# Soft-capped attention, then a max-out MLP, on one core: the scores of the left-over keys are issued ahead of the sums and values, and a third pair of PSUM banks holds scores in the first quad too

## The chip, the cores and the metric

The program runs on one core of one Trainium2 chip. The metric is device time in microseconds, from launch to the end of the program. The profile gives, for one execution, the span from its first to its last instruction. Engines: PE is TensorE's matmul, PEld its weight load, DVE VectorE, ACT ScalarE, POOL GpSimd, SP the engine whose queue issues most DMAs.

## The reference

```python
batch, n_heads, seq, head_dim = 8, 12, 448, 64          # q, k, v, float32
scores = cap * tanh((q @ k.T) / sqrt(64) / cap)          # cap = 30
attn = exp(scores - max(scores)); attn = attn / attn.sum(-1)
attn_out = attn @ v                                      # 8 x 12 x 448 x 64
x = attn_out.transpose(0, 2, 1, 3).reshape(3584, 768)
out = maximum(x @ w1, x @ w2) @ w_out                    # 3584 x 768, d_ff = 1024
```

The kernel leaves the maximum out of the softmax, since the cap bounds the scores. It uses max(a, b) = relu(a - b) + b: `wd_sb` holds w1 - w2, and `wm_sb` holds w2 @ w_out, so that the MLP is relu(x @ wd) @ w_out + x @ wm.

## The kernel before

**Work items.** Two heads of one batch make a pair, two pairs a quad `t` (0 to 23). Heads have 448 keys: three tiles of 128 keys (`j` = 0, 1, 2) and 64 keys that are left over. `scores(t, p)` issues, for pair p = 0 or 1 of the quad, three pairs of matmuls (one of each pair per head, each on half of the array's rows), and each such pair of matmuls fills a pair of PSUM banks that one tanh on ACT (L304) reads. `scores(t, 2)` does the left-over keys of both pairs: the left keys of two heads share one tile of 128, so it is two matmuls (L300), one pair of banks and one tanh. `ex(t, p)` is the exponential (L309) of all the tanhs of that part.

`total(t)` sums the exponentials over the keys with matmuls by a vector of ones (L343 and L347 in the early quads, L350 later), transposes on DVE (L352), takes the reciprocal (L354) and transposes back (L356) into `inv[t]`. `values(t)` is 32 matmuls of 32 columns each (L366, L372), into one pair of banks. `normalize(t, ps)` multiplies both banks by `inv[t]` on DVE (L387), which frees them.

**PSUM.** Eight banks: `s_psum` has two pairs, used in rotation by the scores and by `total`; `v_psum` has one pair, tile name `v`; `mm_psum` has two single banks for the MLP. With `scores(t, p, v_psum)` the third pair of score banks (`j` = 2) is the `v` pair; without it, all three `j` go through the two `s` pairs.

**Order.** It is written out by hand, and every engine runs its own queue in that order. The main loop makes one visit per quad `t`. In a visit the engines get, in this order: `scores(t+1, 0)`, then `ex(t, 2)`, fill, `scores(t+1, 1)`, then `ex(t+1, 0)`, fill, `total(t)`, `values(t)`, `scores(t+1, 2)`, `ex(t+1, 1)`, `normalize(t)`, the POOL casts for a later group, fill. Fill is `F(n)`: the next n matmuls from a queue of MLP work (`moe`, L399, L411 and L414, with DVE evacuations L403 and L418) or, early, of weight work (`turn_w2`, `premultiply`). A full visit calls F for 16 matmuls between the first and the second block of scores, for 24 from there to `total`, and for 5 at the end. What is left of the queue runs after the last visit.

Short names used below: S0, S1 and S2 are the matmuls of `scores(t+1, 0)`, `(t+1, 1)` and `(t+1, 2)`; T0, T1, T2 their tanhs; E0, E1, E2 the exponentials. On ACT a visit is T0, E2 of the quad at hand, T1, E0, T2, E1.

**Inputs.** q, k and v come in groups of three pairs (`load`, issued on SP), are cast to bf16 on POOL (in the visits, behind a copy `mark` at L629 that waits for `inv[t]`), and q and k are then transposed by a DMA (`cross`, L279) into `qkT`. The first two groups are transposed on TensorE instead.

Of the kernel before, what the change touches and what calls it, by code (L numbers as in the profile page):

```python
# [10 lines left out]
def kernel(  # L11
# [41 lines left out]
    v_psum = ctx.enter_context(tc.tile_pool(name="v_psum", bufs=1, space=PSUM))  # L53
# [170 lines left out]
    def subtract(c, eng=nc.vector):  # L224
        eng.tensor_sub(wd_sb[:, c, :], w1_in[c], w2b[:, c, :])
# [35 lines left out]
    def transposes(i):  # L261

        g, n = divmod(i, L)
        ps = mm_psum.tile([P, 512], f32, name="mm").bitcast(bf16)
        x = flat(g)[:, n, :]

        todo = [(j * D, (j % 3) * P + (j // 3) * 64) for j in range(6)]
        odd = i // NP % 2
        todo += [(Q0 + j * D, Q0 + (64 * j if not odd else 0 if j == 6 else 64 + 64 * j)) for j in range(R7)]
        for c, to in todo:  # L270
            for a in range(2):
                r = slice(64 * a, 64 * a + 64)
                nc.tensor.transpose(ps[r, to : to + 64], x[r, c : c + D], ident[r, r])
        nc.tensor.transpose(ps[:, NJ * P : Q0], x[:, NJ * P : Q0], ident)
        nc.vector.tensor_copy(qkT_of(g)[:, n, :, :].rearrange("p j c -> p (j c)")[:, : Q0 + S], ps[:, : Q0 + S])

    def cross(g):

        nc.sync.dma_start_transpose(  # L279
            out=qkT_of(g).rearrange("p n j c -> p (n j) c"), in_=kqf[g % 2].rearrange("p n j c -> p (n j c)")  # L280
        )
# [3 lines left out]
    def two_banks(pool):  # L285
        return pool.tile([P, 2, 512], f32, name="s" if pool is s_psum else "v")

    def scores(t, p, last=None):

        tanh[t, p] = att.tile([P, 2 * NJ, S], bf16, name="tanh")  # L290
        for j in range(NJ if p < 2 else 1):
            s = two_banks(last if last and j == NJ - 1 else s_psum)
            for m in range(2):
                i = 2 * t + (p if p < 2 else m)
                g = i // L
                k0 = qkT[g][:, i % L, :, :].rearrange("p j c -> p (j c)")
                o = Q0 + (64 * (i // NP % 2) if g >= NT else 0)
                qTn = k0[:, o : o + S]
                if p == 2:
                    nc.tensor.matmul(s[:, m, :S], k0[:, 3 * P : 4 * P], qTn)  # L300
                else:
                    r = slice(64 * m, 64 * m + 64)
                    nc.tensor.matmul(s[:, m, :S], k0[r, j * P : (j + 1) * P], qTn[r, :])  # L303
            nc.scalar.activation(tanh[t, p][:, 2 * j : 2 * j + 2, :], s[:, :, :S], AF.Tanh, scale=scale / cap)  # L304

    def ex(t, p):
        n = 2 * NJ if p < 2 else 2
        expo[t, p] = att.tile([P, n, S], bf16, name=f"expo{p}", bufs=2)
        nc.scalar.activation(expo[t, p], tanh[t, p][:, 0:n, :], AF.Exp, scale=float(cap))  # L309

    def e_of(t, ab, j):
        return expo[t, ab][:, 2 * j : 2 * j + 2, :]
# [24 lines left out]
    def total(t):  # L337

        ss = two_banks(s_psum)[:, 0, :]
        if t < NS:  # L340
            for j in range(NJ):
                for ab, h, r in HEADS:
                    nc.tensor.matmul(  # L343
                        ss[r, :S], ones[:, :32], e_of(t, ab, j)[:, h, :], start=(j == 0), stop=False
                    )
            for ab, h, r in HEADS:
                nc.tensor.matmul(ss[r, :S], ones2[:, h, :32], expo[t, 2][:, ab, :], start=False, stop=True)  # L347
        else:
            for ab, h, r in HEADS:
                nc.tensor.matmul(ss[r, :S], ones[:, :32], esum[t][:, 2 * ab + h, :], start=True, stop=True)  # L350
        st = att.tile([P, NB, 32], f32, name="st", bufs=1)
        nc.vector.transpose(st.rearrange("p b c -> p (b c)"), ss[:, :S])  # L352
        rs = att.tile([P, NB, 1], f32, name="rs", bufs=2)
        nc.vector.reciprocal(rs, st[:, :, 0:1])  # L354
        inv[t] = att.tile([P, S], f32, name="inv", bufs=2)
        nc.vector.transpose(inv[t].rearrange("p (b c) -> p b c", c=32), rs.to_broadcast([P, NB, 32]))  # L356

    def values(t):

        out = two_banks(v_psum)  # L360
        for u in range(2):
            ps = out[:, u, :]
            for j in range(NJ):
                for ab, h, r in HEADS:
                    g, n = divmod(2 * t + ab, L)
                    nc.tensor.matmul(  # L366
                        ps[r, :S], vp[g % 2][:, 2 * n + h, j, u::2], e_of(t, ab, j)[:, h, :],
                        start=(j == 0), stop=False,
                    )
            for ab, h, r in HEADS:  # L370
                g, n = divmod(2 * t + ab, L)
                nc.tensor.matmul(  # L372
                    ps[r, :S], vl[g % 2][:, n, 64 * h + u : 64 * h + 64 : 2], expo[t, 2][:, ab, :], start=False, stop=True
                )
        return out
# [3 lines left out]
    def x_of(t, u):  # L379
        b, q = divmod(t, 3)  # L380
        if b // 2 not in xT:
            xT[b // 2] = xpool.tile([P, NP, 2 * S], bf16, name="xT")
        return xT[b // 2][:, 2 * q + u, (b % 2) * S : (b % 2 + 1) * S]

    def normalize(t, ps):
        for u in range(2):
            nc.vector.tensor_mul(x_of(t, u), ps[:, u, :S], inv[t])  # L387
# [55 lines left out]
    def F(n):  # L443
        rate[1] += n * rate[0]
        while rate[1] >= 1 and fill_q:
            try:
                next(fill_q[0])
                rate[1] -= 1
            except StopIteration:
                fill_q.pop(0)  # L450
        if not fill_q:
            rate[1] = 0.0
# [35 lines left out]
    transposes(0)  # L488
    cast(nc.vector, 0, "k", 1, L)
    cast(nc.vector, 0, "q", 1, L)  # L490
    scores(0, 0)
    ex(0, 0)
    transposes(1)
    scores(0, 1)
    ex(0, 1)
    transposes(2)
    for _ in turn_w2(0):
# [35 lines left out]
    def extra(i):  # L533
        for f, a in todo[i]:
            f(*a)

    for _ in turn_w2(1):
        pass
    scores(1, 0)
    transposes(3)  # L540
    cast(nc.vector, 0, "v", halves=(0,))
    cast(nc.gpsimd, 1, "v")
# [28 lines left out]
    for t in range(1, NQ):  # L571
        i = 2 * t
        more = t + 1 < NQ
        if t > 1:
            F(24 if t == 2 else 0)
            if more:
                scores(t + 1, 0, v_psum)
            ex(t, 2)
            F(6)
        if t in crosses:  # L580
            cross(crosses[t])
        if t == 2:
            cast(nc.gpsimd, 3, "k")
            cast(nc.gpsimd, 3, "q")
            cross(3)
            for c in range(4, KC):
                subtract(c, nc.gpsimd)
        if t == 3:
            cast(nc.gpsimd, 3, "v")
        if t > 2:  # L590
            extra(i)
        if t > 1:
            F(2)
            add(t, 0, 0)
            F(3)
            add(t, 0, 1)
            F(3)
            add(t, 1, 0)
            F(2)
        if more:  # L600
            scores(t + 1, 1, v_psum)
            ex(t + 1, 0) if t > 1 else None
        F(3)
        add(t, 1, 1)
        F(4)
        if t == 2:
            cast(nc.gpsimd, 2, "v")
            load(3, "v")
        F(3)
        add(t, 0, 2)  # L610
        F(4)
        add(t, 1, 2)
        if t == 1:
            for c in range(4):
                subtract(c, nc.gpsimd)
        if t == 2:
            extra(4)
            extra(5)
        if t > 2:
            extra(i + 1)  # L620
        F(10)
        total(t)
        ps = values(t)
        if more:
            scores(t + 1, 2)
            ex(t + 1, 1)
        normalize(t, ps)
        if casts[t]:
            nc.gpsimd.tensor_copy(mark, inv[t][:1, :1])  # L629
            for g, what in casts[t]:  # L630
                cast(nc.gpsimd, g, what)
        if t % 3 == 2:
            fill_q.append(moe(t // 3))
        F(5)
# [34 lines left out]
```

## Time and profile before

| | |
|---|---|
| time, median of 3 runs | 371.25 us (370.80 to 371.84) |
| the profiled execution | 372.04 us, of which 370.3 us are its span |
| PE busy | 336.5 us, 91% of the span |
| ACT busy | 277.2 us, 75% |
| DVE busy | 227.2 us, 61% |
| POOL busy | 111.3 us, 30% |
| mean granted TensorE clock | 0.986 |

The visits of quads 3 to 22 begin and end near T2, which starts at 59.57 us for the first of them and at 317.62 us at the end of the last: 20 visits in 258.05 us. What lies ahead of that is the start (loads, transposes, weight work); what lies behind it is the last quad and the rest of the MLP, where ACT has nothing left to do. The share of an engine over the whole span is thus a mean over three quite different stages, and the visits have to be read on their own.

### The profile page before, as it was taken

The page shows a single profiled execution, that of the slowest core. Times are in us where ns is not written, and L with a number is a line of the kernel's source. Part 1 is how long each engine was busy: PE and PEld are TensorE (multiplying, and loading weights), DVE is VectorE, ACT ScalarE, POOL GpSimd, SP SyncE. Part 2 cuts the span into 40 slices and gives each one's busy share as a digit, 9 for nine tenths or more (in the row PEclk, how much of TensorE's full clock was granted, in tenths as well). Part 3 has the DMA queues.
Part 4 walks back from the last instruction along what each step waited for, and adds up shares of the span by engine and source line. Part 5 has one row for each costly group of instructions (what it writes and reads, how often), then busy time and mean ns, then how long its engine had stood idle before and what let it go on. Part 6 is the DMA issues. An engine that isn't in the chain of part 4 may idle for free.

```text
span 370.3 us, 6777 instructions
## 1 busy us (share of the span) xinstructions
PE 336.5 (91%) x2710; PEld 167.3 (45%) x2710; DVE 227.2 (61%) x410; ACT 277.2 (75%) x241; POOL 111.3 (30%) x172
## 2 busy tenths in 40 slices
PE   3679989999999998999999999999999999999996
PEld 2334544444444444454444444444444544455563
DVE  4225637857687655766676666867587666863421
ACT  3997677798889889788988988798898889500000
POOL 6652938324404421430332143034204400000000
PEclk9958999999999999999999999999999999999999
DMA  7999998984984399448946796759783512012022
GB/s 255 245 248 258 315 242 164 267 195 111 225 273 86 118 232 307 97 111 184 304 115 145 153 293 182 163 95 253 206 193 65 139 44 87 2 42 87 0 87 85
DMA packets 103199, 61.78 MB, mean 167 GB/s; under 512 B 62336, under 2 KB 98176, under 8 KB 103168
## 3 DMA queue, kind: packets, MB, share of 16 engines
q1 hardware_dynamic: 101216, 58.21, 60.8%
q0 software_dynamic: 1952, 3.15, 4.7%
q8 instruction: 21, 0.34, 0.4%
q14 instruction: 10, 0.08, 0.1%
HBM read 42.47 MB, written 11.01 MB: 144 GB/s over the span
## 4 chain that ended last, share of the span: by engine, by line
PE 52%; ACT 29%; DMA 12%; DVE 3%; issue 2%; SPq 0%; ACTq 0%; DVEq 0%
ACT tanh L304 17%; PE mm L414 14%; ACT expo L309 11%; PE mm L399 11%; PE mm L411 10%; DMA kr<-in_k_dram 8%; PE v L366 6%; DMA qkT<-kqf 3%; PE s L300 3%; PE v L303 2%; PE v L372 2%; PE s L350 2%; PE mm L243 2%; DMA osb<-in_moe_w_dram 1%; DVE gT L403 1%
## 5 line engine op out<-in xcount | busy, mean ns | idle before, releaser
L304 ACT ACTIVATE tanh<-s 128x896 bf16<-128x896 f32 x125 | 108.8, 914 | 43.0 <-PE s L300 33.4
L309 ACT ACTIVATE expo<-tanh 128x2688 bf16<-128x2688 bf16 (+1 forms) x72 | 140.3, 1950 | 0.8 <-PE v L366 0.6
L414 PE MATMUL mm<-wo_sb,gT 128*128 128x384 bf16 x448 | 85.5, 326 | 0.0
L399 PE MATMUL mm<-xT,wd_sb 128*128 128x448 bf16 x384 | 78.3, 353 | 0.8 <-DVE gT L403 0.7
L411 PE MATMUL mm<-wm_sb,xT 128*128 128x384 bf16 x336 | 65.8, 326 | 0.0
L418 DVE COPY osb<-mm 128x384 f32<-128x384 f32 x56 | 31.1, 555 | 56.5 <-PE mm L414 55.2
L414 PEld LDWEIGHTS <-gT 128*128 128x128 bf16 x448 | 42.8, 98 | 31.3 <-issue 3.6
L399 PEld LDWEIGHTS <-wd_sb 128*128 128x128 bf16 x384 | 36.5, 98 | 37.8 <-issue 6.1
L403 DVE TENSOR_SCALAR gT<-mm 128x448 bf16<-128x448 f32 x64 | 39.5, 621 | 19.9 <-PE mm L399 19.5
L303 PE MATMUL s<-qkT 64*128 64x448 bf16 x202 | 35.7, 373 | 15.9 <-ACT tanh L304 12.0
L629 POOL COPY mark<-inv 1x1 f32<-1x1 f32 x18 | 3.2, 178 | 154.3 <-DVE inv L356 137.0
L411 PEld LDWEIGHTS <-xT 128*128 128x128 bf16 x336 | 32.0, 98 | 24.2 <-issue 3.4
L303 PEld LDWEIGHTS <-qkT 64*128 64x128 bf16 x288 | 13.7, 94 | 58.6 <-issue 52.6
L304 ACT ACTIVATE tanh<-v 128x896 bf16<-128x896 f32 x43 | 39.7, 923 | 0.0
L366 PE MATMUL v<-expo,vp 128*32 128x448 bf16 x576 | 35.6, 353 | 0.0
L387 DVE TENSOR_TENSOR xT<-v,inv 128x448 bf16<-128x448 f32 x48 | 27.7, 619 | 4.7 <-PE v L372 2.0
L327 DVE TENSOR_TENSOR esum<-esum,expo 64x896 bf16<-64x896 bf16 x42 | 26.2, 623 | 7.1 <-ACT expo L309 6.4
L329 DVE TENSOR_TENSOR esum<-expo 128x896 bf16<-128x896 bf16 x42 | 28.3, 674 | 0.0
L331 DVE TENSOR_TENSOR esum<-esum,expo 128x896 bf16<-128x896 bf16 x42 | 26.8, 637 | 0.8
L352 DVE STREAM_TRANSPOSE st<-s 128x448 f32<-128x448 f32 x24 | 15.6, 649 | 17.7 <-PE s L350 15.9
L303 PE MATMUL v<-qkT 64*128 64x448 bf16 x86 | 15.6, 351 | 8.9 <-ACT tanh L304 8.9
L366 PEld LDWEIGHTS <-vp 128*32 128x32 bf16 x576 | 15.3, 97 | 10.0
(66 smaller groups left out, 258.5 us busy)
## 6 DMA issues: line engine op xcount, KB each, us to landing
kr<-in_k_dram SPq DMA_DIRECT2D x14, 576.0 KB, 6.8
qr<-in_q_dram SPq DMA_DIRECT2D x14, 576.0 KB, 6.9
vr<-in_v_dram SPq DMA_DIRECT2D x14, 576.0 KB, 5.0
out_dram<-osb SPq DMA_DIRECT2D x20, 384.0 KB, 4.2
out_dram<-osb SPq DMA_DIRECT2D x16, 192.0 KB, 3.5
osb<-in_moe_w_dram SPq DMA_DIRECT2D x4, 512.0 KB, 8.6
gT<-in_moe_w_dram POOLq DMA_DIRECT2D x6, 256.0 KB, 12.6
wo_sb<-in_moe_w_out_dram POOLq DMA_DIRECT2D x4, 384.0 KB, 16.1
```

What stands on the lines that cost most here:

```text
L303: nc.tensor.matmul(s[:, m, :S], k0[r, j * P : (j + 1) * P], qTn[r, :])
L304: nc.scalar.activation(tanh[t, p][:, 2 * j : 2 * j + 2, :], s[:, :, :S], AF.Tanh, scale=scale / cap)
L309: nc.scalar.activation(expo[t, p], tanh[t, p][:, 0:n, :], AF.Exp, scale=float(cap))
L329: nc.vector.tensor_add(d, e_of(t, ab, 0), e_of(t, ab, 1))
L331: nc.vector.tensor_add(d, d, e_of(t, ab, 2))
L366: nc.tensor.matmul(ps[r, :S], vp[g % 2][:, 2 * n + h, j, u::2], e_of(t, ab, j)[:, h, :], start=(j == 0), stop=False,)
L387: nc.vector.tensor_mul(x_of(t, u), ps[:, u, :S], inv[t])
L399: nc.tensor.matmul(ps[:, :S], wd_sb[:, c, f * P : (f + 1) * P], x[:, c, cs], start=(c == 0), stop=(c == KC - 1))
L403: nc.vector.tensor_relu(g[:, f, cs], ps[:, :S])
L411: nc.tensor.matmul(ps[:, : DM // 2], x[:, c, ts], wm_sb[:, c, hs], start=(c == 0), stop=False)
L414: nc.tensor.matmul(ps[:, : DM // 2], g[:, f, ts], wo_sb[:, f, hs], start=False, stop=(f == FC - 1))
L418: nc.vector.tensor_copy(osb[:, hs], ps[:, : DM // 2])
```

## The change

In every visit `scores(t+1, 2)` and its exponential's issue move ahead of `total(t)` and `values(t)`, and `normalize(t)` follows them directly. Separately, three of the scores in the start use the `v` pair for `j` = 2.

```diff
@@ the first quad
-    scores(0, 0)
+    scores(0, 0, v_psum)
     ex(0, 0)
     transposes(1)
-    scores(0, 1)
+    scores(0, 1, v_psum)
...
-    scores(1, 0)
+    scores(1, 0, v_psum)
...
@@ the end of a visit
         F(10)
-        total(t)
-        ps = values(t)
         if more:
             scores(t + 1, 2)
             ex(t + 1, 1)
-        normalize(t, ps)
+        total(t)
+        normalize(t, values(t))
         if casts[t]:
```

On TensorE the left-over scores (L300, into an `s` pair) are found, in the changed program, behind the fill and ahead of the sums. The piece shown is from the visit of quad 2, whose fill is weight work (L243) and whose sums are L343.

```order
 L243 LDWEIGHTS w2T
 L243 MATMUL mm<-wo_sb,w2T 128x384 [waits DVE_49]
+L300 LDWEIGHTS qkT
+L300 MATMUL s<-qkT 128x448 [waits Activation_49]
+L300 LDWEIGHTS qkT
+L300 MATMUL s<-qkT 128x448
 L343 LDWEIGHTS ones
 L343 MATMUL s<-expo_527,ones 32x448 [waits Activation_49]
```

The four rows stood behind the last matmul of the values (L372) before; in the rotation of the `s` pairs they now take the pair that the sums took, and the sums the other.

The next place is S0 of a visit, the first scores behind the values, on TensorE. First the rows before: `s` is a pair of `s_psum`, `v` the pair of `v_psum`, and the waits are on semaphores that ACT, DVE, a DMA or PE itself raise.

```order
L303 LDWEIGHTS qkT [waits DMAHW2_49]
L303 MATMUL s<-qkT 128x448 [waits DVE_49]
L303 LDWEIGHTS qkT
L303 MATMUL s<-qkT 128x448
L303 LDWEIGHTS qkT
L303 MATMUL s<-qkT 128x448 [waits Activation_49]
L303 LDWEIGHTS qkT
L303 MATMUL s<-qkT 128x448
L303 LDWEIGHTS qkT
L303 MATMUL v<-qkT 128x448 [waits DVE_49]
```

And the same rows of the changed program.

```order
L303 LDWEIGHTS qkT [waits DMAHW2_49]
L303 MATMUL s<-qkT 128x448 [waits Activation_49]
L303 LDWEIGHTS qkT
L303 MATMUL s<-qkT 128x448
L303 LDWEIGHTS qkT
L303 MATMUL s<-qkT 128x448 [waits DVE_49]
L303 LDWEIGHTS qkT
L303 MATMUL s<-qkT 128x448
L303 LDWEIGHTS qkT [waits DVE_49]
L303 MATMUL v<-qkT 128x448 [waits PE_49]
```

The first pair of S0 waited for the transpose of the sums on DVE and now waits for T2 on ACT; the second has it the other way round; the third waits for `normalize` on DVE in both, now at the weight load.

The third place is the start, on TensorE: the weight product into the `v` pair (L521, `premultiply_first`) between the scores of pairs (1, 0) and (1, 1).

```order
-L521 LDWEIGHTS w2T
-L521 MATMUL v<-wo_sb,w2T 128x384 [waits DMASW2_49]
+L521 LDWEIGHTS w2T [waits DMASW2_49]
+L521 MATMUL v<-wo_sb,w2T 128x384 [waits Activation_49]
 L521 LDWEIGHTS w2T
 L521 MATMUL v<-wo_sb,w2T 128x384
```

It now waits, besides the weights' DMA, for the tanh on ACT that reads the `v` pair of `scores(1, 0)`.

## The prediction, made before the changed kernel was run

> **What bounds the kernel now.** I read the page's engine shares and slices first, then three stretches of the trace by themselves, then who waits for whom, then one visit in order of time.
>
> The page's shares over the whole span, and its row of the granted clock in 40 slices:
>
> ```profile
> PE 336.5 (91%) x2710; PEld 167.3 (45%) x2710; DVE 227.2 (61%) x410; ACT 277.2 (75%) x241; POOL 111.3 (30%) x172
> PEclk9958999999999999999999999999999999999999
> ```
>
> Two stretches: the start, and the 20 visits (length, then busy time of each engine with its instructions, the granted clock, the DMA engines' share, GB/s):
>
> ```profile
> 0.00:48.97 48.97, 35.41 (x397) 18.66 (x398) 21.28 (x48) 35.18 (x30) 29.40 (x45) 0.90 1.06 259
> 64.10:317.60 253.50, 237.23 (x1876) 113.80 (x1876) 174.94 (x308) 225.20 (x197) 72.13 (x117) 1.00 0.67 171
> ```
>
> The start is full on the DMA side (share 1.06). In the visits PE is busy 237.2 of 253.5 us and ACT 225.2: both near full, neither quite. So each waits for the other somewhere. The waits, with total, times and longest:
>
> ```profile
> ACT tanh L304 <- PE s L300: 33.4, 23, 3.4
> PE s L303 <- ACT tanh L304: 12.0, 20, 1.6
> PE v L303 <- ACT tanh L304: 8.9, 20, 0.4
> PE mm L399 <- DVE gT L403: 0.7, 3, 0.3
> ```
>
> ACT waits for the left-over scores, which stand behind sums and values on PE; PE waits at S1 for the tanhs that free the banks. Is that a closed loop? ACT's T2 at the first visit, in the middle and at the last one:
>
> ```profile
> 59.57 0.92 ACT L304 ACTIVATE tanh<-s 128x896 bf16<-128x896 f32 x1 [1.87 <-PE s L300]
> 124.13 0.92 ACT L304 ACTIVATE tanh<-s 128x896 bf16<-128x896 f32 x1 [1.09 <-PE s L300]
> 317.62 0.92 ACT L304 ACTIVATE tanh<-s 128x896 bf16<-128x896 f32 x1 [1.54 <-PE s L300]
> ```
>
> Between the first and last there are 20 visits, 258.05 us, 12.90 each. PE through one of them (start, duration):
>
> ```profile
> 121.66 0.37 PE L350 MATMUL s<-esum,ones 128*32 128x448 bf16 x4
> 123.48 0.55 PE L300 MATMUL s<-qkT 128*128 128x448 bf16 x2
> 123.87 0.81 PE L414 MATMUL mm<-wo_sb,gT 128*128 128x384 bf16 x4
> 124.78 0.69 PE L303 MATMUL s<-qkT 64*128 64x448 bf16 x4
> 125.29 0.37 PE L303 MATMUL v<-qkT 64*128 64x448 bf16 x2
> 125.59 0.99 PE L411 MATMUL mm<-wm_sb,xT 128*128 128x384 bf16 x5
> 128.38 0.36 PE L303 MATMUL s<-qkT 64*128 64x448 bf16 x2
> 129.19 0.36 PE L303 MATMUL s<-qkT 64*128 64x448 bf16 x2 [0.44 <-ACT tanh L304]
> 130.00 0.36 PE L303 MATMUL v<-qkT 64*128 64x448 bf16 x2 [0.45 <-ACT tanh L304]
> 130.29 0.66 PE L411 MATMUL mm<-wm_sb,xT 128*128 128x384 bf16 x3
> 134.30 0.37 PE L350 MATMUL s<-esum,ones 128*32 128x448 bf16 x4
> ```
>
> From sum to sum 12.64 us. It is a loop: T2, E1 and T0 on ACT free S1's banks; PE then does 24 fill matmuls, sums, values and S2, and only then can T2 start again. In it ACT loses 1.09 us, so its own work is 11.55 us a visit.
>
> **The change: S2 ahead of the sums.** No instruction is added or removed in a visit.
>
> On ACT, S2 would be issued where the sums start now, 121.66, and E0 ends 1.09 us before 124.13, at 123.04. T2 then follows E0 with no wait. S2's bank comes free with the first tanh of T1; it is the bank that the sums take now, and their row at 121.66 has no wait. The sums then need the second tanh of T1, and the values, as now, the third.
>
> On PE, S1's second and third pair no longer wait, since T0 comes that much earlier. What a wait costs is read from starts, since the ends are modelled. Six score matmuls without a wait:
>
> ```profile
> 111.23 1.11 PE L399 MATMUL mm<-xT,wd_sb 128*128 128x448 bf16 x5
> 112.28 0.55 PE L303 MATMUL s<-qkT 64*128 64x448 bf16 x4
> 112.66 0.35 PE L303 MATMUL v<-qkT 64*128 64x448 bf16 x2
> 112.95 0.55 PE L399 MATMUL mm<-xT,wd_sb 128*128 128x448 bf16 x2
> ```
>
> First to third pair: 0.38 us, all six 0.67. In the visit above S1 takes 1.62 to the third pair: 1.24 us lost, more than the gaps of 0.44 and 0.45, because pairs that run apart don't overlap. The first and the last S1 of the 20:
>
> ```profile
> 64.11 0.36 PE L303 MATMUL s<-qkT 64*128 64x448 bf16 x2
> 65.44 0.36 PE L303 MATMUL v<-qkT 64*128 64x448 bf16 x2 [0.45 <-ACT tanh L304]
> 308.79 0.37 PE L303 MATMUL s<-qkT 64*128 64x448 bf16 x2
> 310.40 0.36 PE L303 MATMUL v<-qkT 64*128 64x448 bf16 x2 [0.44 <-ACT tanh L304]
> ```
>
> 0.95 and 1.23. Taken so, 14 of the 20 lose 1.19 to 1.24, five whose fill before S1 is L399 lose 0.78 to 0.90, and the first 0.95: **22.6 us** in all.
>
> S0 has a small wait too: in the visit above its third pair comes 0.51 after the first, not 0.38. The second pair waits for T2, which starts at 124.13 and ends at 125.05. That bank is then the sums' and early, and S0's first pair, which takes T2's bank, finds it free: 0.13 in 14 visits, **1.8 us**.
>
> Against these stands a wait that grows. S0's third pair needs the `v` banks, which `normalize` frees:
>
> ```profile
> 122.09 0.65 DVE L352 STREAM_TRANSPOSE st<-s 128x448 f32<-128x448 f32 x1 [1.39 <-PE s L350]
> 123.87 1.16 DVE L387 TENSOR_TENSOR xT<-v,inv 128x448 bf16<-128x448 f32 x2
> 127.41 1.73 ACT L304 ACTIVATE tanh<-s 128x896 bf16<-128x896 f32 x2
> ```
>
> `normalize` ends at 125.03, 3.37 after the sums start; with the 0.05 between the end of T0's second tanh (129.14) and the matmul that waits for it (129.19), 3.42. S2 (123.48 to 123.87, 0.39) no longer lies between, so PE reaches that pair 1.82 (sums, values) + 0.91 (five fill matmuls) + 0.38 = 3.11 after it: 0.31 of wait. Where the five are L399 (111.23 to 112.28, 1.05) it is 0.17; that is six visits. 14 x 0.31 + 6 x 0.17 = **5.4 us**. Bounds: nothing, if the weight load ahead covers it; another 20 x 0.65 = 13 us, if DVE came to the sums late by as much as L352 itself takes. DVE stood idle 1.39 us there, so I stay at the computed value.
>
> Behind the waiting pair stand the 16 fill matmuls and S1; they are part of the same 0.31.
>
> Does ACT keep up? PE's new visit is 0.67 + 0.31 + 2.79 (125.59 to 128.38) + 0.67 + 4.01 (130.29 to 134.30) + 0.39 + 1.82 + 0.91 = 11.57 us against ACT's 11.55: a tie in visits with L411 and L414, PE longer in the others. T0 has all of S0's tail and 2.79 us of fill, over 3 us, before S1 asks for its first banks, so a small lag of ACT costs nothing.
>
> DVE in the L399 visits: three waits of PE for gT, 0.7 us, are there now. With the rest pulled together, the longest of them, 0.3, in each of six visits makes 1.8; none if the adds on DVE come earlier with E2. I take 0.8.
>
> POOL and SP: the sums and `inv` move back by 0.39, and with them POOL's casts and the transposing DMA:
>
> ```profile
> 123.83 0.18 POOL L629 COPY mark<-inv 1x1 f32<-1x1 f32 x1 [8.62 <-DMA vr<-in_v_dram]
> 128.31 3.67 SPq L279 DMA_TRANSPOSE qkT<-kqf  x1
> qkT<-kqf SPq DMA_TRANSPOSE x14, 5.6
> ```
>
> Issued at 128.31, it lands near 133.9; the next S0 is at 124.78 + 12.64 = 137.42. That leaves 3.5 us, of which 0.39 and one visit's gain of 1.1 go: 2.0 remain. Free.
>
> **The change: three uses of `v` in the start.** PE's waits for tanh in `scores(0, 0)`, `(0, 1)` and `(1, 0)` go. But the visits begin at a wait for a DMA:
>
> ```profile
> 48.97 0.55 PE L303 MATMUL s<-qkT 64*128 64x448 bf16 x4 [1.12 <-DMA qkT<-kqf]
> 38.70 10.23 DMA qkT<-kqf
> 18.48 2.51 ACT L304 ACTIVATE tanh<-s 128x896 bf16<-128x896 f32 x3
> 20.40 1.49 PE L521 MATMUL v<-wo_sb,w2T 128*128 128x384 bf16 x4
> ```
>
> The transposing DMA from 38.70 lands at 48.93 whatever PE did before, so the gain here is nothing. The added wait: L521 needs the tanh that ends at 20.99 and starts at 20.40 now, so 0.6 later, beside an exponential and with 1.12 us of slack at 48.97. Its bounds are therefore 0 and, if it ran through, 0.6 of loss. I take 0 for the whole edit.
>
> **Sum.** 22.6 + 1.8 - 5.4 - 0.8 = **18.2 us** of gain. The profiled execution took 372.04 (span 370.3), which becomes 353.8; it is 0.8 above the median of the three runs, 371.25, which becomes **353.0**. The tail behind 317.6 keeps its length, since the number of fill matmuls in the visits is the same.
>
> **Rivals.** *`normalize` comes later than computed.* In each visit S0 loses another 0.5: 10 us less gain, 363. For it: 0.31 is a difference of sums over two engines, and the weight load too waits there now. Against: DVE idle before L352.
>
> *ACT alone sets the visits.* Then every visit shrinks to 11.55: 258.05 - 231.0 = 27 us of gain, 344. For it: 33.4 us of waits are ACT's. Against: the L399 fill is PE time that no wait explains. The Trainium skill's Perfetto Trace Analysis (Identifying the Most-Contended Engine) says that matmul busy time misjudges TensorE and that occupancy is fair for ScalarE; by it ACT is the engine to free and the sum would be 344. The start-to-start times of PE disagree: its work without waits adds up to 11.57.
>
> *The stall only moves.* If S2 finds its bank busy, PE stands ahead of the sums as long as it did in S1: 371. Against: the sums take that same bank now, and at 121.66 their row shows no wait.
>
> *Slower.* The `v` loop decides: values, `normalize`, S0's third pair. If L352 starts more than 1.2 us later after the sums than now (DVE behind with evacuations as PE runs denser), 20 visits lose more than the 24.4 gained; at 1.5 it is 377. Against it stand the idle 1.39 and only 0.7 us of PE's waits for gT.
>
> **Numbers.** Forecast 0.66 (its own range 349.5 to 357); late `normalize` 0.16 (357 to 367); ACT alone 0.06; stall moved 0.06; slower 0.06. The range 348.5 to 360.5 takes in the forecast and most of the nearer part of late `normalize`. A measurement of this kernel tells about 0.3% from no change. Faster 0.88, same 0.06, slower 0.06.
>
> **What would show it.** After: ACT's wait for L300 gone from the visits; PE's wait for tanh at L303 near zero there; a wait of L303 for DVE xT of 0.2 to 0.3 in most visits; T2 every 11.6 us, 12.5 in L399 visits; ACT now waits for S0 or S1 in the latter; the first S0 for `qkT` by DMA still near 49 us. I am wrong if the `v` wait exceeds 0.6, if S1 still waits for T0, or if the granted clock of the visits leaves 1.00.

## The result, and the profile after

The changed kernel takes 352.89 us in the median of four runs (352.48 to 354.52), against 371.54 for the kernel before on the same chip: a ratio of 0.951, 95% interval 0.947 to 0.954. A second comparison gave 0.949 (0.946 to 0.951). The forecast was 353.0, faster. The profiled execution took 352.48 us, 350.7 of it span: 19.6 us less span, where the sum had said 18.2 less.

The page's shares after the change. PE is now busy 94% of the span:

```profile
PE 329.2 (94%) x2710; PEld 163.3 (47%) x2710; DVE 228.6 (65%) x410; ACT 277.2 (79%) x241; POOL 113.3 (32%) x172
PEclk9959999999999999999999999999999999999999
```

The waits (total, times, longest), for the same pairs as before, and the new one of S0 for `normalize`:

```profile
ACT tanh L304 <- PE s L300: 4.7, 9, 1.0
ACT tanh L304 <- PE s L303: 14.4, 10, 6.5
PE s L303 <- ACT tanh L304: 3.0, 2, 2.0
PEld L303 <- DVE xT L387: 10.8, 21, 0.9
PE mm L399 <- DVE gT L403: 0.8, 2, 0.6
```

ACT's wait for the left-over scores fell from 33.4 to 4.7 us. PE's 8.9 us for the third pair is gone from the list, and of its 12.0 for the others 3.0 are left, in two waits of the start. The weight load of S0's third pair now waits for `normalize` in 21 places; its idle time begins before PE is free, so the price has to be read from the matmuls. One visit of PE, with fill of L411 and L414:

```profile
116.86 0.54 PE L300 MATMUL s<-qkT 128*128 128x448 bf16 x2
117.34 0.37 PE L350 MATMUL s<-esum,ones 128*32 128x448 bf16 x4
119.16 0.82 PE L414 MATMUL mm<-wo_sb,gT 128*128 128x384 bf16 x4
120.08 0.55 PE L303 MATMUL s<-qkT 64*128 64x448 bf16 x4
120.75 0.36 PE L303 MATMUL v<-qkT 64*128 64x448 bf16 x2
121.05 0.99 PE L411 MATMUL mm<-wm_sb,xT 128*128 128x384 bf16 x5
123.76 0.55 PE L303 MATMUL s<-qkT 64*128 64x448 bf16 x4
124.14 0.35 PE L303 MATMUL v<-qkT 64*128 64x448 bf16 x2
128.34 0.54 PE L300 MATMUL s<-qkT 128*128 128x448 bf16 x2
```

From S2 to S2 the visit takes 11.48 us, where it took 12.64. S1 (123.76 to 124.14) runs without a gap. S0's third pair comes 0.67 after its first, not 0.38: that is the wait for the `v` banks, 0.29. On ACT and DVE around the same visit:

```profile
115.16 2.46 ACT L309 ACTIVATE expo<-tanh 128x2688 bf16<-128x2688 bf16 x1
117.64 0.92 ACT L304 ACTIVATE tanh<-s 128x896 bf16<-128x896 f32 x1
129.22 0.92 ACT L304 ACTIVATE tanh<-s 128x896 bf16<-128x896 f32 x1
119.54 1.16 DVE L387 TENSOR_TENSOR xT<-v,inv 128x448 bf16<-128x448 f32 x2
```

T2 starts 0.02 after E0 ends, with no wait, and ACT needs 11.58 us from T2 to T2. `normalize` ends at 120.70, 3.36 after the sums began, and the third pair starts at 120.75.

Added up over the visits of quads 3 to 22 in both traces, by starts:

| us over the 20 visits | before | after |
|---|---|---|
| first S2 to last S2 | 258.05 | 238.47 |
| S1, lost between first and third pair | 22.6 | 0.2 |
| S0, the same | 1.9 | 5.25 |

22.4 less in S1 and 3.3 more in S0 make 19.1 of the 19.6 us. The first pair of S1 adds 0.9: from the start of the fill matmul ahead of it to its own start 6.3 us pass in the 20 visits before, and 5.4 after. Against it, the stretch now begins ahead of quad 2's sums, which are 16 matmuls in place of 4 and take 0.55 more. Ahead of the first S2 the kernel is 2.3 us shorter and behind the last 2.3 longer, which cancels: S2 itself now stands earlier in its visit.

### The profile page after: what moved, and what is told of

Same layout as the page of the kernel before. It is cut to its first block, busy times and chain, and to the rows that moved or that the text cites. A ratio compares the mean times of both kernels' runs of the same rounds, so it can differ in the third digit from the quotient of the medians.

```text
span 350.7 us, 6777 instructions
## 1 busy us (share of the span) xinstructions
PE 329.2 (94%) x2710; PEld 163.3 (47%) x2710; DVE 228.6 (65%) x410; ACT 277.2 (79%) x241; POOL 113.3 (32%) x172
## 4 chain that ended last, share of the span: by engine, by line
PE 73%; DMA 13%; DVE 10%; issue 2%; SPq 0%; DVEq 0%
PE mm L414 20%; PE mm L399 19%; PE mm L411 15%; DMA kr<-in_k_dram 9%; PE s L303 4%; PE v L366 4%; DVE xT L387 3%; PE v L303 3%; DMA qkT<-kqf 3%; PE s L300 2%; PE mm L243 2%; PE s L350 2%; DVE st L352 2%; DVE inv L356 2%; DMA osb<-in_moe_w_dram 1%
## 5 line engine op out<-in xcount | busy, mean ns | idle before, releaser
L304 ACT ACTIVATE tanh<-s 128x896 bf16<-128x896 f32 x122 | 106.4, 914 | 21.1 <-PE s L303 14.4
L414 PE MATMUL mm<-wo_sb,gT 128*128 128x384 bf16 x448 | 85.6, 327 | 0.0
L399 PE MATMUL mm<-xT,wd_sb 128*128 128x448 bf16 x384 | 78.5, 353 | 1.0 <-DVE gT L403 0.8
L411 PE MATMUL mm<-wm_sb,xT 128*128 128x384 bf16 x336 | 65.9, 326 | 0.0
L414 PEld LDWEIGHTS <-gT 128*128 128x128 bf16 x448 | 42.3, 98 | 33.6 <-issue 7.5
L418 DVE COPY osb<-mm 128x384 f32<-128x384 f32 x56 | 31.1, 555 | 40.8 <-PE mm L414 40.6
L399 PEld LDWEIGHTS <-wd_sb 128*128 128x128 bf16 x384 | 35.9, 98 | 39.2 <-issue 8.9
L411 PEld LDWEIGHTS <-xT 128*128 128x128 bf16 x336 | 31.7, 98 | 25.1 <-issue 5.1
L304 ACT ACTIVATE tanh<-v 128x896 bf16<-128x896 f32 x46 | 42.5, 923 | 0.0
L303 PE MATMUL s<-qkT 64*128 64x448 bf16 x196 | 29.1, 371 | 7.8 <-ACT tanh L304 3.0
L329 DVE TENSOR_TENSOR esum<-expo 128x896 bf16<-128x896 bf16 x42 | 29.3, 698 | 0.0
L303 PEld LDWEIGHTS <-qkT 64*128 64x128 bf16 x288 | 10.5, 95 | 38.7 <-issue 19.8
L327 DVE TENSOR_TENSOR esum<-esum,expo 64x896 bf16<-64x896 bf16 x42 | 26.1, 622 | 1.4
L183 POOL CAST kqf<-kr 128x1152 bf16<-128x1152 f32 x14 | 15.9, 1138 | 10.4 <-DMA kr<-in_k_dram 10.1
```

Of the source, the lines that this page charges most:

```text
L329: nc.vector.tensor_add(d, e_of(t, ab, 0), e_of(t, ab, 1))
L399: nc.tensor.matmul(ps[:, :S], wd_sb[:, c, f * P : (f + 1) * P], x[:, c, cs], start=(c == 0), stop=(c == KC - 1))
L411: nc.tensor.matmul(ps[:, : DM // 2], x[:, c, ts], wm_sb[:, c, hs], start=(c == 0), stop=False)
L414: nc.tensor.matmul(ps[:, : DM // 2], g[:, f, ts], wo_sb[:, f, hs], start=False, stop=(f == FC - 1))
L418: nc.vector.tensor_copy(osb[:, hs], ps[:, : DM // 2])
```

## The experiments

**Which part of the change.** The first kernel has the visits changed and the start as before; the second has the start changed alone.

```diff
-    scores(0, 0, v_psum)     # and (0, 1), (1, 0); visits as in the changed kernel
+    scores(0, 0)
```

> The left-over scores ahead of the sums in every visit, and the start as before. If the visits carry the whole gain: 353 us, within 0.3% of the changed kernel, ratio to before near 0.950. If the three uses of the v pair in the start carry some of it: more than 354.5 us.

```diff
-    scores(0, 0)             # and (0, 1), (1, 0); visits as in the kernel before
+    scores(0, 0, v_psum)
```

> Only the three uses of the v pair in the start. If the transposing DMA that lands near 49 us sets the beginning of the visits: 371 us, no change, and the first scores out of that DMA still start near 49 us, with PE waiting longer ahead of them. If the start's waits for tanh were on the path: 368 to 370 us.

The visits alone: 351.95 us, ratio 0.947 (0.945 to 0.949). The start alone: 372.22, ratio 1.002 (1.000 to 1.003). The whole gain is in the visits; the 0.2% between the visits alone and the changed kernel is within the intervals. In the kernel with only the start changed, the DMA and PE at the first scores of the visits:

```profile
38.96 10.31 DMA qkT<-kqf
49.31 0.55 PE L303 MATMUL s<-qkT 64*128 64x448 bf16 x4 [2.50 <-DMA qkT<-kqf]
```

PE comes there 1.0 us earlier and waits 2.50 us instead of 1.12. The DMA lands no earlier for it, at 49.27 (48.93 before).

**Is the loss a closed loop?** If T2, E1, T0, S1's banks, 24 fills, sums, values and S2 form the loop, then ACT has free time ahead of T2 in the old order and not in the new, and PE has free time ahead of S1 in the old order. Four kernels add work to one place each. The first puts a small exponential on ACT in the changed kernel:

```diff
+    idle = const.tile([P, 64], bf16, name="idle")
...
             ex(t + 1, 0) if t > 1 else None
+            nc.scalar.activation(idle, ones, AF.Exp)
```

> The changed kernel, and one more small exponential on ACT in each visit (64 columns, about 0.27 us), behind E0; its output is not used. If ACT and PE are tied in the visits with L411 and L414 fill: each of some 14 visits grows by about 0.25 us, 356 to 357 us in all. If PE alone sets the visits: 353 us. If ACT alone sets them all: 20 times 0.27, 358 us or more.

352.45 us, 0.949 (0.945 to 0.954): no change, which is the number of the reading that PE alone sets the visits. But the test was too weak to tell the readings apart. ACT in that kernel, E0, the added operation, T2:

```profile
115.29 2.46 ACT L310 ACTIVATE expo<-tanh 128x2688 bf16<-128x2688 bf16 x1
117.62 0.27 ACT L604 ACTIVATE idle<-ones 128x64 bf16<-128x64 bf16 x1
117.78 0.92 ACT L305 ACTIVATE tanh<-s 128x896 bf16<-128x896 f32 x1
```

T2 starts 0.03 after E0's end, as without it (0.02): the 0.27 us lie beside the end of the exponential and the start of the tanh. So a larger one, in both kernels:

```diff
+    idle = const.tile([P, 2, S], bf16, name="idle")
...
             ex(t + 1, 0) if t > 1 else None
+            if t > 1:
+                nc.scalar.activation(idle, tanh[t + 1, 0][:, 0:2, :], AF.Exp, scale=float(cap))
```

> The changed kernel with one more exponential of 896 columns (0.96 us, some 0.85 behind its neighbour) on ACT in each visit, between E0 and T2; its output is not used. ACT's work becomes 12.4 us a visit, PE's is 11.92 in the mean. If ACT has only 0.35 us a visit to spare: 360 to 364 us, and PE waits for tanh at S1. If ACT is not near the path: 353 us.

> The kernel before with the same extra exponential of 896 columns on ACT in each visit, between E0 and T2; its output is not used. In the old order ACT waits 1.09 to 2.15 us for the left-over scores just there, so if the wait lies in a closed loop whose PE part (fill, sums, values, S2) sets T2's start, the 0.85 us cost nothing: 370 to 373 us. If ACT's load as such set the visits: 388 us.

On the changed kernel: 362.54 us, 0.976 (0.973 to 0.978), some 10 us more. On the kernel before: 371.73, 0.999 (0.997 to 1.002), nothing. Their waits, the changed kernel first, then the kernel before:

```profile
ACT tanh L305 <- PE s L301: 1.3, 2, 0.9
PE v L304 <- ACT tanh L305: 4.9, 12, 0.4
```

```profile
ACT tanh L305 <- PE s L301: 15.7, 23, 3.4
PE v L304 <- ACT tanh L305: 8.9, 20, 0.4
```

In the old order the added 0.87 us only shortens ACT's wait, from 33.4 to 15.7. In the new order ACT has little left, and PE stands at S1 again (10.0 us between first and third pairs, by starts).

The fourth adds fill on PE between S2 and S0 in the old order:

```diff
-        F(5)
+        F(8)
```

> The kernel before, old order, with eight fill matmuls in place of five between S2 and S0 (three more in each visit, taken from the tail). They lie outside the loop, where T2, E1 and T0 run on ACT and PE would stand at S1 later. If PE's stall at S1 is free time: visits as long as now, PE's 3 x 20 matmuls of 0.163 to 0.194 us leave the tail, 360 to 363 us. If PE's order is full and each adds its time: 371 us.

361.38 us, 0.971 (0.968 to 0.973). From first to last S2 257.4 us pass, with 52 more matmuls in them (60 by the edit, but in one visit the fill queue ran dry); the loss at S1 fell from 22.6 to 14.4 us and S0's from 1.9 to 0.2. PE's stall was free time, and the tail got shorter by what moved in.

**Is it the order as such?** The old order, with the loop shortened on PE's side:

```diff
             add(t, 1, 0)
-            F(2)
+            F(9)
...
-        F(10)
+        F(3)
         total(t)
```

> The kernel before, in its old order, with seven of the 24 fill matmuls between the second block of scores and the sums moved ahead of that block, to where PE waits for the tanhs. Nothing else changes. If the loss was the closed loop (T2, E1, T0, S1's banks, 24 fills, sums, values, S2), the loop gets 7 x 0.163 = 1.1 us shorter, ACT's own 11.55 us or PE's work sets the visits, and the time is 350 to 355 us without any reordering. If the place of the left-over scores as such is what counts: 370 to 372 us.

360.44 us, 0.970 (0.967 to 0.974): between the two readings. S1's loss went to 2.0 us without a reordering, so the loop is confirmed, but the visits shrank to 244.1 us, not 238.5. A second wait took the rest, which the expectation had not named. PE and DVE at the sums of one visit:

```profile
250.08 0.56 DVE L418 COPY osb<-mm 128x384 f32<-128x384 f32 x1 [1.19 <-PE mm L414]
250.62 0.36 PE L350 MATMUL s<-esum,ones 128*32 128x448 bf16 x1
250.65 0.62 DVE L327 TENSOR_TENSOR esum<-esum,expo 64x896 bf16<-64x896 bf16 x1
251.32 0.37 PE L350 MATMUL s<-esum,ones 128*32 128x448 bf16 x3 [0.34 <-DVE esum L327]
253.14 0.55 PE L300 MATMUL s<-qkT 128*128 128x448 bf16 x2
```

DVE's last add (L327) stands here in DVE's queue behind the evacuation of fill (L418), which waits for PE. With only 17 fill matmuls between S1 and the sums, the first of the four sums starts, and the other three wait until that add has ended, at 251.27. From the sums to S2 2.52 us pass here, where 1.82 passed before. In 16 of the 20 visits the second sum starts 0.18 to 0.73 us behind the first, each time about 0.05 after the end of that add; before, all four started within 0.01. Sums and values together take 6.7 us more over the 20 visits. The 20.6 us saved at S1, less these 6.7, are the 13.9 by which the visits shrank.

**The wait that is left.** Four kernels more: the changed one again, two that should remove S0's wait for `normalize`, and one that lengthens it.

> The changed kernel once more, beside the next kernels on the same chip: 353 us, ratio 0.950.

352.64 us, 0.949 (0.946 to 0.951).

```diff
         F(10)
+        total(t)
         if more:
             scores(t + 1, 2)
             ex(t + 1, 1)
-        total(t)
         normalize(t, values(t))
```

> The left-over scores between the sums and the values (sums, S2, values) instead of ahead of both. DVE's work on the sums then runs 0.4 us ahead of PE's next scores, and S0's wait for normalize, 5.25 us over the visits of the changed kernel, should vanish. If PE's waits are what is left to gain: 347 to 349 us. If ACT (11.55 us of work a visit) already sets the visits with L411 and L414 fill: 351 to 353 us, and PE waits for the tanhs at S1 again.

352.21 us, 0.948 (0.945 to 0.950): no gain, though S0's loss fell from 5.3 to 0.9 us and S1's stayed at 0.2. Neither expectation holds: the time lies in the range of the second, but PE doesn't wait at S1, as it should have by that one. PE in that kernel:

```profile
117.69 0.37 PE L350 MATMUL s<-esum,ones 128*32 128x448 bf16 x4
118.00 0.55 PE L300 MATMUL s<-qkT 128*128 128x448 bf16 x2
118.48 0.75 PE L366 MATMUL v<-expo,vp 128*32 128x448 bf16 x12
120.11 0.82 PE L414 MATMUL mm<-wo_sb,gT 128*128 128x384 bf16 x4
```

The sums take 0.31 from start to start, where they take 0.20 when the values follow; S2 takes 0.48, and took 0.39 when fill followed. Each change between matmuls that use 128 columns of the array and 32 columns costs about 0.1 us, and this order has two more of them in a visit. In the mean of the 20 visits, the step from fill to the sums takes 0.265 us, where the step from fill to S2 takes 0.172 in the changed kernel; the step from the sums to S2 takes 0.296, where the one from the sums to the values takes 0.189. That is 0.20 us a visit, 4.0 in all, and S0 had saved 4.4: the visits with L411 and L414 fill take 11.45 to 11.48 us, as before.

```diff
-        F(5)
+        F(7)
     F(10 ** 9)
```

> The changed kernel with seven fill matmuls in place of five between the values and S0 (taken from the tail, where nothing waits). 2 x 0.163 = 0.33 us of work then lies where PE waits 0.30 for normalize. If only PE's idle time counts: 347 to 349 us, visits as long as now, the tail some 6 us shorter. If the two matmuls make each visit longer and nothing is hidden: 353 us.

348.30 us, 0.938 (0.935 to 0.941): 1.2% faster than the changed kernel, and the fastest here. The time is the expected one, its parts are not quite. A visit of it on PE:

```profile
117.76 0.54 PE L300 MATMUL s<-qkT 128*128 128x448 bf16 x2
121.29 0.55 PE L303 MATMUL s<-qkT 64*128 64x448 bf16 x4
121.68 0.35 PE L303 MATMUL v<-qkT 64*128 64x448 bf16 x2
129.26 0.54 PE L300 MATMUL s<-qkT 128*128 128x448 bf16 x2
```

The third pair follows after 0.39, and the visit takes 11.50 us with two matmuls more. But all 20 take 242.6 us, 4.2 more than in the changed kernel, where no more was expected: 36 matmuls came into them (40 by the edit, but in one visit the fill queue ran dry), 31 of them L399, and the visits with L399 grew. The tail is 8.0 shorter.

```diff
+    late = const.tile([P, S], f32, name="late")
...
     def normalize(t, ps):
+        nc.vector.tensor_copy(late, ps[:, 0, :S])
```

> The changed kernel with one more DVE copy (128 x 448 float32, about 0.62 us) ahead of normalize in each visit; its output is not used. If normalize frees the v pair on the path, S0's wait grows from 0.30 to 0.9 us in 20 visits: 364 to 366 us. If ACT's lag or spare time covers it: 353 us.

361.15 us, 0.969 (0.966 to 0.972), less than expected. The copy, then `normalize`, and S0's third pair in that kernel:

```profile
123.66 0.59 DVE L387 COPY late<-v 128x448 f32<-128x448 f32 x1
124.16 1.14 DVE L389 TENSOR_TENSOR xT<-v,inv 128x448 bf16<-128x448 f32 x2
125.36 0.36 PE L304 MATMUL v<-qkT 64*128 64x448 bf16 x2 [0.44 <-DVE xT L389]
```

`normalize` now ends 3.67 after the sums' start (121.63), 0.31 later and not 0.62: the copy starts 2.03 after the sums, where `normalize` started 2.20 after them, and `normalize` follows 0.50 behind it. S0's loss grew by 6.0 us (5.3 to 11.3), and the 20 visits by 6.3: what delays `normalize` there is paid in full. Another 2.3 us lie in the start; there the transposing DMA landed 1.05 later than in the changed kernel (50.19, 49.14), and what part the copy has in it is not shown.

## Why the prediction was right

*S1, 22.6 us.* Measured 22.4. Reading the loss from starts rather than from the gaps mattered: the gaps shown at S1 in the 20 visits add up to about two thirds of it, 15.2 us.

*S0, -5.4 and +1.8.* After the change S0 loses 5.25 us, predicted 5.4; before it lost 1.9. The visits split as computed: 0.10 to 0.17 in the six with L399 behind the values, 0.23 to 0.30 in 13 others. One visit lost 0.65, just beyond the 0.6 that was named as a sign of being wrong; there `normalize` itself began 2.56 after the sums, not 2.20. The others lost a little less than computed and made up for it in the sum. The added copy and the added fill show the same wait growing and going.

*DVE in the L399 visits, -0.8.* This term was mis-sized: PE waits 0.8 us for gT in all, 0.7 before, and the longest of them, 0.6, now lies in the tail. Without it the sum is 19.0 against 19.6 of span. The sum also had no term for the first pair of S1, worth 0.9. Both misses point the same way, and the span fell by 1.4 more than the sum. That the median came within 0.1 us of the forecast is therefore in part luck: the profiled execution of the kernel before was a slower one than its median, that of the changed kernel a faster one.

*ACT and PE tied.* Right in the visits with L411 and L414 fill: PE 11.48, ACT 11.58. ACT falls behind by 0.1 a visit and regains it in the L399 visits, where it still waits up to 1.0 us for L300 and, as forecast, up to 0.6 for L303 (from 57 us on 3.6 and 2.5 us, seven waits each). The forecast that the wait for L300 would go altogether was therefore too strong. That ACT's spare time is short was shown only by the larger exponential.

*The start, 0.* Right, by the DMA: it lands at 49.14 in the changed kernel, 48.93 before, and PE waits 2.68 us for it. L521's wait for the tanh was put at 0.6 us; PE waits 1.4 in the kernel after, and it is hidden all the same.

*The rivals.* ACT alone would have given visits of 11.55 us, 231.0 in all, and 344 us; they take 238.5. In the kernel with seven fills the visits grew by 4.2 us with ACT's work unchanged, so PE's time counts. The Trainium skill's rule (Perfetto Trace Analysis, Identifying the Most-Contended Engine) that points to ACT's occupancy did not give the time here: ACT ends at 79% of the span. A stall that only moves is excluded by the row of S2 at 116.86, which has no wait. The late `normalize` exists as a mechanism at 0.29 us a visit, not at 0.8. The kernel with the added copy, 0.31 later, still beats the one before. The sum of the slower case left out the 6.2 us (5.4 and 0.8) that the forecast takes off already: with them, a DVE 0.9 us later, not 1.2, would have eaten the 24.4, and 1.5 later would give 383 us, not 377. No run delayed `normalize` by that much.

## What to carry to other kernels

Where two engines each show waits for the other and neither is full, follow one round of the loop through both: the gain of a reordering is the stall read from start to start on the engine that is near its limit, minus what the moved work no longer covers. The work to move out of such a loop is the work nobody in it needs, and the place to put spare work is in front of the wait that is left: two fill matmuls there gave another 1.2%. Moving spare work can open a second wait, as the sums' wait for DVE did when the fill ahead of them was cut to 17. Then test each engine's spare time by adding work to it, and make the addition large enough not to hide beside its neighbour.

## What the runs showed of the hardware

A change between matmuls on 128 columns and on 32 columns of the array cost PE about 0.1 us (0.31 against 0.20, 0.48 against 0.39). In the changed kernel the weight loads of S2 and of the sums start as follows:

```profile
116.70 0.26 PEld L300 LDWEIGHTS <-qkT 128*128 128x128 bf16 x2
117.33 0.10 PEld L350 LDWEIGHTS <-ones 128*32 128x32 bf16 x4 [0.37 <-issue]
```

Behind fill of its own form S2's load starts 0.16 ahead of its matmul (116.86). The sums' load starts 0.01 ahead of theirs (117.34), and in all 20 visits the load at this change starts at most 0.01 ahead. Where a 128x128 matmul follows another, it starts at least 0.16 ahead.

The Trainium skill, TensorEngine Tiling (Array Packing), Key Properties, says that a change of tiling mode drains TensorE; the rows agree, and give the price that it leaves open.

A 0.27 us exponential between E0 and T2 on ACT moved T2 by 0.01 us against E0's end (0.03, and 0.02 without it): in the rows above it starts 0.13 before E0 ends, and T2 starts 0.11 before it ends. One of 896 columns, 0.96 us long, moved T2 to 0.87 after E0's end.
